# Attention and a top-1 mixture of experts on one core: token rows read in quarters and block-transposed by VectorE, reads on the sync queue, empty slots zeroed ahead

## The chip, the cores and the metric

One core of a Trainium2 chip runs the whole program. The metric is the device time of one execution in microseconds; the kernel before has three such runs. TensorE (PE) multiplies matrices, VectorE (DVE) and ScalarE (ACT) work on elements, GpSimd (POOL) issues the indirect DMAs, whose rows are chosen by an index, and SyncE (SP) issues the plain ones. The engines run side by side, each takes its own instructions in order, and they wait for each other on semaphores.

## The reference

```python
kv  = einsum('bhsd,bhse->bhde', k, v)            # 8 batches, 8 heads, 576 positions, 64 wide
o   = einsum('bhsd,bhde->bhse', q, kv)
o   = o / sqrt(mean(o*o, -1) + 1e-6) * g_norm
x   = o.transpose(0, 2, 1, 3).reshape(4608, 512)  # tokens x channels
logits = x @ w_gate                               # 8 experts
e   = argmax(logits);  p = softmax(logits)[e]
out[t] = p[t] * (relu(x[t] @ w1[e[t]]) @ w2[e[t]])  # w1: 512 x 1024, w2: 1024 x 512
```

Inputs and output are float32. Each token goes to one expert only.

## The kernel before, in words

**Attention.** A loop runs over the eight batches and one round more. A round forms `kv` of its batch (`kv_mm`), transposes the queries on PE (`t_mm`), folds the gate weights into the right operand (`fold_mm`) and copies it to SBUF (`x_copy`). Between these pieces it works on tiles of 128 tokens of the batch pair before: nine tiles a pair, four pairs, 36 tiles. A tile is a product on PE (`o_mm`), the mean of squares on ACT and DVE (`o_red`), its root (`o_nrm`), and the scaling into a row of `xrow` (`o_x`, L676 the rows, L680 the logits). A row is 516 16-bit words: 512 channels in float16, the gate value and the token's number. Row buffers hold three tiles each, and there are four of them.

**Routing.** `route(j, t0, t1)` works on a chunk of tiles of pair j, by generator steps between the tiles of attention. It finds the expert of each token and its place among that expert's tokens, and scatters the rows by an indirect DMA on POOL (L743) into the DRAM array `x_slots`, in which each expert has room for all tokens. The counts go from chunk to chunk.

**Experts.** The slots of an expert are taken in groups of tiles: g0 to g2 are the first three tiles of experts 0 to 2, g3 to g5 the last two tiles of the same, g6 to g10 five tiles each of experts 3 to 7. A spill group for what an expert has beyond its five tiles is put in before the last group, and a loop for still more (`For_i`) at the end has a count that is zero with these inputs. A group is fetched by `fetch`, one indirect gather a tile on POOL (L291), into one of three row buffers `xl`. Slots that no token has taken are out of bounds for the gather, and the buffers were zeroed once at the start. `xpose` turns a tile's four 128x128 blocks on PE (L325), and DVE evicts the result times `g_norm` (L328). `stage1` (L345) takes eight steps of 128 hidden units, with the Relu on ACT (L353); `stage2` (L361) makes one tile of output, DVE scales it by the gate value (L366), and POOL scatters it to the output (L369). The gathers of group r+2 are issued in the first step of stage 1 of group r, and the transposes of r+1 stand between the tiles of stage 2 of r.

**Weights.** Each expert's w1 and w2 come as eight loads of 512 KB on SP's queue (`w_load`, L206 and L210) into four staging buffers, and DVE casts them to float16 (`w_cast`, L220). `w_step` does one cast and one load; its calls are written out by hand between the steps of attention and of the groups.

**Order.** The order of the instructions is that of the program: there is no planner. Buffers come from pools with a number of copies per tag, and the framework puts in the semaphore waits: a tile or DRAM array that is read waits for its writers, and one that is written waits for its readers. `dram_disjoint_views` declares slices whose writers need not wait for each other. The last eight groups are issued by the loop `while unit()`, and the first ones in between attention, from the fourth tile of the last round.

```python
for k in range(cur.K):
    cur.stage2(k)
    if not cur.small:
        w_step()
    while todo and len(todo) > max(cur.K - 2 - k, 0):
        nxt.xpose(todo.pop(0))
```

Of the kernel before, what the change touches and what calls it, by code (L numbers as in the profile page):

```python
# [45 lines left out]
def kernel(  # L46
# [20 lines left out]
    xs_views = dram_disjoint_views(xs.ap(), NT)  # L67
# [9 lines left out]
    for j in range(4):  # L77
# [20 lines left out]
        "w1off": arf[:, None] + 128.0 * np.array([0, 2, 1, 3], np.float32)[None, :],  # L98
# [36 lines left out]
    nc.scalar.dma_start(g2[64:128, :], g_norm.unsqueeze(1))  # L135
    wgt = P_const.tile([128, 8, 8], F32, tag="wgt")
# [17 lines left out]
    chunks = {0: [(0, 9)], 1: [(0, 9)], 2: [(0, 3), (3, 9)], 3: [(0, 3), (3, 6), (6, 9)]}  # L154
    ohbs, n_route = [], 0
    for j in range(4):
# [7 lines left out]
    xl_ring = [  # L164
        P_const.tile([128, SLOT_TILES, ROW], I16, tag=f"xl{n}", name=f"xl{n}") for n in range(3)
    ]
# [13 lines left out]
    def w_load(pool, bufs):  # L180
# [23 lines left out]
        if n < 4:  # L204
            r0 = 128 * (2 * (n % 2) + n // 2)
            nc.sync.dma_start(st, w1[r0 : r0 + 128, :])  # L206
            dst = w_tiles[e][0][:, n, :]
        else:
            m = 2 * (n - 4)
            nc.sync.dma_start(  # L210
                st.rearrange("p (t d) -> p t d", t=2),
                w2[128 * m : 128 * m + 256, :].rearrange("(t p) d -> p t d", p=128),
            )
            dst = w_tiles[e][1][:, m : m + 2, :].rearrange("p t d -> p (t d)")
        w_staged.append((e, dst, st))

    def w_cast(engine):
        if w_staged:
            e, dst, st = w_staged.pop(0)
            engine.tensor_copy(dst, st)  # L220
# [5 lines left out]
    def w_step():  # L226
        if len(w_staged) == 4 or not w_todo:
            w_cast(nc.vector)
# [8 lines left out]
    cnt = P_const.tile([128, 8], F32, tag="cnt")  # L237
    srow = P_const.tile([128, 8, SLOT_TILES], F32, tag="srow")
# [4 lines left out]
    def row_index(name, ctr, ne, nk):  # L243
        bad = P_const.tile([128, ne, nk], F32, tag="bad" + name, name="bad" + name)
        nc.vector.tensor_tensor(
            bad, _bc(cv["srank"][:, 0:nk], 1, ne), _bc(ctr[:, 0:ne], 2, nk), op=ALU.is_ge
        )
        idx = P_const.tile([128, ne, nk], I32, tag="idx" + name, name="idx" + name)
        nc.vector.scalar_tensor_tensor(
            out=idx, in0=bad, scalar=BIG, in1=srow[:, 0:ne, 0:nk], op0=ALU.mult, op1=ALU.add  # L250
        )
        badi = P_const.tile([128, ne, nk], I32, tag="badi" + name, name="badi" + name)
        nc.vector.tensor_scalar(badi, bad, BIG, None, op0=ALU.mult)
        return idx, badi

    rows = {}

    def early_rows():
        ctr = P_const.tile([128, 8], F32, tag="cnt_e")
        b0 = base[len(routed)]  # L260
        nc.vector.tensor_tensor(ctr, b0, cv["ebase"], op=ALU.subtract)
        rows["early"] = row_index("e", ctr, EARLY, EARLY_TILES)
        nc.vector.tensor_tensor(b0, b0, cv["efloor"], op=ALU.max)
        yield
        for i in range(EARLY):
            groups[i].fetch()
        yield

    def final_rows():
        nc.vector.tensor_tensor(cnt, base[n_route], cv["ebase"], op=ALU.subtract)  # L270
        rows["all"] = row_index("a", cnt, 8, SLOT_TILES)

    class Group:
        def __init__(self, n, e, k0, k1):
# [4 lines left out]
            self.xl = xl_ring[n % 3]  # L279
            self.table = "early" if self.small and k0 == 0 else "all"  # L280

# [6 lines left out]
        def fetch(self):  # L288
            idx = rows[self.table][0]
            for k in range(self.K):  # L290
                nc.gpsimd.indirect_dma_start(  # L291
                    out=self.xl[:, k, :], out_offset=None, in_=xs.ap(),
                    in_offset=IndirectOffsetOnAxis(
                        ap=idx[:, self.e, self.k0 + k : self.k0 + k + 1], axis=0
                    ),
                    bounds_check=E * N - 1, oob_is_err=False,
                )

        def slot_ids(self):
            badi = rows[self.table][1]  # L300
# [3 lines left out]
                self.xl[:, 0 : self.K, D + 2 : D + 4].bitcast(I32),  # L304
                badi[:, self.e, self.k0 : self.k0 + self.K].unsqueeze(2), op=ALU.max,
            )

# [6 lines left out]
        def start(self):  # L314
            self.xsT = self.pool().tile(
                [128, 4, self.n], F16, tag="xsT" + self.tag(), bufs=1, name="xsT"
            )

        def tag(self):
            return ""  # L320

        def xpose(self, k):
            ps = PSA.tile([128, 4, 128], F16, tag="KV", bufs=2, name="xps")
            for c in range(4):
                nc.tensor.transpose(  # L325
                    ps[:, c, :], self.xl[:, k, c * 128 : (c + 1) * 128].bitcast(F16), ident16
                )
            nc.vector.tensor_scalar(  # L328
                self.xsT[:, :, k * 128 : (k + 1) * 128], ps, g2, None, op0=ALU.mult
            )  # L330

        def stage1(self, f):
            if f == 0:
                self.hT = self.pool().tile(
                    [128, 8, self.n], F16, tag="hT" + self.tag(), bufs=1, name="hT"
# [7 lines left out]
            for kk in range(4):  # L343
                for hp, s in zip(hps, starts):
                    nc.tensor.matmul(  # L345
                        hp,
                        self.w()[0][:, kk, f * 128 : (f + 1) * 128],
                        self.xsT[:, kk, s : s + self.step],
# [6 lines left out]
        def stage2(self, k):  # L355
            if self.small:
                yp = PSA.tile([128, D], F32, tag="O", bufs=2, name="yp")
            else:
                yp = PSA.tile([128, D], F32, tag="T", bufs=2, name="yp")
            for f in range(8):  # L360
# [6 lines left out]
                y, yp, self.xl[:, k, D : D + 2].bitcast(F32), None, op0=ALU.mult  # L367
# [10 lines left out]
    class SpillGroup(Group):  # L378
        def __init__(self, tables, col, view):
            self.tables, self.col, self.view = tables, col, view  # L380
            self.e, self.K, self.n, self.step, self.small = "s", 1, 128, 128, False

        def tag(self):
            return "d"
# [25 lines left out]

    class LoopGroup(SpillGroup):
# [3 lines left out]
        def fetch(self):  # L415
            super().fetch()
            self.wd = (
# [73 lines left out]
    tabs = []  # L491
# [4 lines left out]
    def ffn():  # L496
        order = list(groups)
        cur = order[0]
# [394 lines left out]
```

## Time and profile before

| what | value |
| --- | --- |
| runs, median (lowest to highest) | 352.06 us (350.06 to 354.91) |
| the profiled execution | 330.94 us |
| its span, first to last instruction | 329.2 us |
| mean granted PE clock | 0.903 |
| busy: PE, DVE, ACT, POOL | 269.0, 183.4, 119.9, 137.6 us |
| stage 1 starts: g0, g1, g2, g3 | 153.1, 169.1, 180.5, 191.7 us |
| stage 1 starts: g6, g7, g8, g9, g10 | 221.9, 240.4, 258.9, 277.3, 302.7 us |

The runs were timed in another session than the profile; the profiled execution is 6% below their median. Sums made from the profile are made against 330.94 us. In the page, a busy time is that of an engine; an idle time is given with what ended it; the clock row is the share of full speed that PE was granted, in forty slices of 8.2 us. A row of groups ends with the idle time ahead of the group and the instruction that released it.

### The profile page before, as it was taken

To read this page: it belongs to the slowest core of one execution; us is meant where nothing else is said; L and a number is where in the kernel's file an instruction comes from. 1 tells how busy PE (TensorE), PEld (TensorE's weight loads), DVE (VectorE), ACT (ScalarE), POOL (GpSimd) and SP (SyncE) were. 2 spreads that over 40 slices of the span, in tenths; PEclk is the share of its full clock that TensorE was granted. 3 is DMA by queue.
4 is the path that set the end of the run, shared out by engine and by line. 5 is a ranking of instruction groups with operands and counts; after the bars stand their busy time and mean duration, and the time that the engine had idled before them with its cause. 6 is when DMAs were issued, how large, how long until landed. Compare 5 with 4: busy or idle time off the path is not lost.

```text
span 329.2 us, 7247 instructions
## 1 busy us (share of the span) xinstructions
PE 269.0 (82%) x2759; PEld 189.3 (58%) x2759; DVE 183.4 (56%) x433; ACT 119.9 (36%) x316; POOL 137.6 (42%) x147
## 2 busy tenths in 40 slices
PE   0699897689766977564979996989999999997980
PEld 0587776577656866462535563657565665645630
DVE  6205566346745368889184678344657658375040
ACT  1136564436543445322322431326142240602600
POOL 9100001720076004384675462777477656052041
PEclk9999997959995589555999998999999999999996
DMA  6999999997897016799589894667799999983021
GB/s 158 334 368 367 369 368 367 381 282 216 246 323 295 18 67 167 250 323 324 201 260 372 295 322 121 214 214 251 250 339 358 351 397 279 408 284 130 0 99 55
DMA packets 45395, 85.79 MB, mean 261 GB/s; under 512 B 6188, under 2 KB 22829, under 8 KB 45360
## 3 DMA queue, kind: packets, MB, share of 16 engines
q1 hardware_dynamic: 36736, 66.07, 59.9%
q0 software_dynamic: 6976, 18.96, 15.6%
q10 hardware_dynamic: 1648, 0.29, 0.5%
q8 instruction: 22, 0.36, 0.4%
q14 instruction: 13, 0.11, 0.1%
HBM read 71.77 MB, written 15.50 MB: 265 GB/s over the span
## 4 chain that ended last, share of the span: by engine, by line
PE 26%; issue 11%; DMA 9%; POOL 7%; DVE 5%; POOLq 1%; ACT 0%; DVEq 0%; ACTq 0%
PE hp L345 13%; PE yp L361 11%; DMA out_dram<-y,d_id 7%; POOL out_dram L369 4%; POOL xl L291 2%; DMA xl<-x_slots,idxe 2%; PE xps L325 1%; DVE y L366 1%; DMA x_slots<-xrow,posi 1%; POOL x_slots L743 1%; DVE w1e L220 1%; DVE xsT L328 0%; POOLq L888 0%; POOLq L854 0%; DVE w2e L220 0%
## 5 line engine op out<-in xcount | busy, mean ns | idle before, releaser
L353 ACT ACTIVATE hT<-hp 128x320 f16<-128x320 f32 (+3 forms) x136 | 53.6, 426 | 106.5 <-PE hp L345 105.9
L345 PE MATMUL hp<-xsT,w1e 128*128 128x320 f16 (+2 forms) x512 | 76.6, 306 | 7.2 <-DVE xsT L328 6.3
L361 PE MATMUL yp<-w2e,hT 128*128 128x512 f16 x320 | 74.1, 379 | 0.3 <-DVE y L366 0.3
L369 POOL DMA_INDIRECT out_dram<-y,idv x40 | 44.6, 1115 | 60.3 <-DVE y L366 49.3
L345 PEld LDWEIGHTS <-w1e 128*128 128x128 f16 x512 | 51.0, 100 | 32.1 <-issue 11.7
L651 PE MATMUL ops<-kvx,qT 64*128 64x72 f32 (+1 forms) x640 | 48.0, 310 | 10.5 <-DVE lhat L680 9.6
L743 POOL DMA_INDIRECT x_slots<-xrow,posi x36 | 35.7, 991 | 40.5 <-DVE xrow L739 15.5
L651 PEld LDWEIGHTS ops<-kvx,qT 64*128 64x128 f32 (+1 forms) x640 | 42.3, 215 | 15.0 <-issue 9.3
L361 PEld LDWEIGHTS <-hT 128*128 128x128 f16 x328 | 30.8, 98 | 31.6 <-issue 0.4
L366 DVE TENSOR_SCALAR y<-yp,xl 128x512 f32<-128x512 f32 x40 | 30.0, 750 | 33.6 <-PE yp L361 29.9
L664 DVE TENSOR_REDUCE ms<-sq 128x8 f32<-128x512 f32 x36 | 24.6, 685 | 25.1 <-ACT sq L660 25.0
L291 POOL DMA_INDIRECT xl<-x_slots,idxa x31 | 32.4, 1046 | 11.7 <-issue 7.0
L594 PE MATMUL kvps<-mk,mv 128*64 128x64 f32 x640 | 28.7, 258 | 9.4 <-DMA mv<-in_v_dram 9.1
L676 DVE TENSOR_TENSOR xrow<-ops,rs 128x512 f16<-128x512 f32 x36 | 24.7, 686 | 18.0 <-DMA x_slots<-xrow,posi 9.3
L660 ACT ACTIVATE sq<-ops 128x512 f32<-128x512 f32 x36 | 21.5, 598 | 31.9 <-PE ops L651 31.5
L594 PEld LDWEIGHTS kvps<-mk,mv 128*64 128x64 f32 x640 | 26.0, 168 | 11.8 <-issue 10.3
L710 POOL COPY xrow<-tokc 128x3 int32<-128x3 int32 x12 | 3.0, 253 | 64.3 <-DVE xrow L676 64.2
L582 PE MATMUL tps<-ctile,mq 128*128 128x128 f32 x144 | 26.9, 320 | 3.5 <-ACT qT L583 1.9
L220 DVE CAST w2e<-wst 128x1024 f16<-128x1024 f32 x32 | 22.3, 704 | 11.4 <-DMA wst<-in_moe_w_dram 11.4
L583 ACT COPY qT<-tps 128x384 f32<-128x384 f32 x48 | 21.9, 473 | 14.4 <-PE tps L582 14.4
L328 DVE TENSOR_SCALAR xsT<-xps,g 128x512 f16<-128x512 f16 x41 | 19.2, 477 | 12.9 <-PE xps L325 12.7
L220 DVE CAST w1e<-wst 128x1024 f16<-128x1024 f32 x32 | 21.6, 688 | 4.5 <-DMA wst<-in_moe_w_dram 4.5
(99 smaller groups left out, 184.1 us busy)
## 6 DMA issues: line engine op xcount, KB each, us to landing
wst<-in_moe_w_dram SPq DMA_DIRECT2D x64, 512.0 KB, 5.8
mq<-in_q_dram SPq DMA_DIRECT2D x16, 576.0 KB, 7.8
mk<-in_k_dram SPq DMA_DIRECT2D x16, 320.0 KB, 7.5
mv<-in_v_dram SPq DMA_DIRECT2D x16, 320.0 KB, 7.3
mk<-in_k_dram SPq DMA_DIRECT2D x16, 256.0 KB, 7.9
mv<-in_v_dram SPq DMA_DIRECT2D x16, 256.0 KB, 7.1
wsts<-in_moe_w_dram SPq DMA_DIRECT2D x8, 512.0 KB, 5.9
out_dram<-y,idv POOLq DMA_INDIRECT x40, 4.9
```

Source lines behind the costliest of these rows:

```text
L220: engine.tensor_copy(dst, st)
L291: nc.gpsimd.indirect_dma_start(out=self.xl[:, k, :], out_offset=None, in_=xs.ap(), in_offset=IndirectOffsetOnAxis(ap=idx[:, self.e, self.k ...
L345: nc.tensor.matmul(hp, self.w()[0][:, kk, f * 128 : (f + 1) * 128], self.xsT[:, kk, s : s + self.step], start=(kk == 0), stop=(kk == 3),)
L353: nc.scalar.activation(self.hT[:, f, s : s + self.step], hp, ACTF.Relu)
L361: nc.tensor.matmul(yp, self.hT[:, f, k * 128 : (k + 1) * 128], self.w()[1][:, f, :], start=(f == 0), stop=(f == 7),)
L366: nc.vector.tensor_scalar(y, yp, self.xl[:, k, D : D + 2].bitcast(F32), None, op0=ALU.mult)
L369: nc.gpsimd.indirect_dma_start(out=self.views(k), out_offset=IndirectOffsetOnAxis(ap=self.ids[:, k : k + 1], axis=0), in_=y, in_offset=Non ...
L582: nc.tensor.transpose(ps[:, c, :], src[:, 128 * m : 128 * m + 128], cv["ident"])
L594: nc.tensor.matmul(kvps[b][64 * y : 64 * y + 64, 2 * u + a, :], main["v", b, u][:, 2 * y + a, c, :], main["k", b, u][:, 2 * y + a, c, :], ...
L651: nc.tensor.matmul(ps[p0 : p0 + 64 * n, y, o0 : o0 + 72], qT[b][hs, a, blk // 2 : blk // 2 + n, :].rearrange("d c p -> d (c p)"), kvx[b][h ...
L676: nc.vector.tensor_tensor(xr[:, 0:D].bitcast(F16).rearrange("p (a h d) -> p a h d", a=2, h=4), xv, _bc(rs2, 3, 64), op=ALU.mult,)
L743: nc.gpsimd.indirect_dma_start(out=xs_views[9 * j + t0 + t], out_offset=IndirectOffsetOnAxis(ap=posi[:, t : t + 1], axis=0), in_=xrow[j, ( ...
```

## The change

1. The gathers on POOL are replaced. `fetch` reads an expert's slots by place: four plain DMAs on SP's queue, each of which brings one quarter of the channels of all rows (pieces of 256 bytes) to 32 partitions, and a fifth that brings gate values and token numbers (`gi`). Since slots that no token has taken are now read too, `pads` writes rows of zeros to them ahead of it, by one indirect scatter a tile on POOL, out of bounds for the slots that are taken.
2. `xpose` is one transpose in 32x32 blocks on DVE for a whole group. w1's rows are loaded in the order that fits (`(p c) f -> c p f`), and the scale by `g_norm` is put into the casts of w1.
3. The early groups' zeroing follows pair 1 (`early_pads`), closed by a small read on POOL's queue (`fence`); the fetches of groups 0 and 1 follow chunk (2, 9), that of group r+2 follows the first tile of stage 2 of group r, and `pads` of group r+3 follows the first step of stage 1 of group r. The transpose of r+1 follows the second tile of stage 2 of r.
4. Pair 2 is routed in chunks (0,6), (6,9) instead of (0,3), (3,9); there are six row buffers instead of four; `x_copy` is on ACT alone; the experts' steps begin with the second tile of the last round; casts in the last two rounds of attention are shared with ACT.
5. The count of the loop at the end is read in stage 1 of g7, and a memset at the end is gone.

```diff
-    chunks = {0: [(0, 9)], 1: [(0, 9)], 2: [(0, 3), (3, 9)], 3: [(0, 3), (3, 6), (6, 9)]}
+    chunks = {0: [(0, 9)], 1: [(0, 9)], 2: [(0, 6), (6, 9)], 3: [(0, 3), (3, 6), (6, 9)]}
...
-            nc.sync.dma_start(st, w1[r0 : r0 + 128, :])
+            nc.sync.dma_start(st, w1.rearrange("(p c) f -> c p f", c=4)[n])
...
+            if engine is nc.scalar:
+                if n < 4:
+                    engine.mul(dst, st, g4[:, n : n + 1])
+                else:
+                    engine.copy(dst, st)
+            elif n < 4:
+                engine.tensor_scalar(dst, st, g4[:, n : n + 1], None, op0=ALU.mult)
+            else:
+                engine.tensor_copy(dst, st)
...
+    def early_pads():
...
+        for g in groups[0:EARLY]:
+            g.pads()
+            yield
+        fence = P_const.tile([1, 4], I16, tag="fence")
+        nc.gpsimd.dma_start(fence, xs.ap()[0:1, D:ROW])
...
     def early_rows():
...
+        groups[0].fetch()
         yield
-        for i in range(EARLY):
-            groups[i].fetch()
+        yield
+        groups[1].fetch()
         yield
...
     def final_rows():
...
+        for n in range(EARLY, EARLY + 2):
+            groups[n].pads()
...
-        def fetch(self):
-            idx = rows[self.table][0]
+        def pads(self):
+            pad = pads[self.table]
             for k in range(self.K):
                 nc.gpsimd.indirect_dma_start(
-                    out=self.xl[:, k, :], out_offset=None, in_=xs.ap(),
-                    in_offset=IndirectOffsetOnAxis(
-                        ap=idx[:, self.e, self.k0 + k : self.k0 + k + 1], axis=0
+                    out=self.pad_views[k],
+                    out_offset=IndirectOffsetOnAxis(
+                        ap=pad[:, self.e, self.k0 + k : self.k0 + k + 1], axis=0
                     ),
+                    in_=zrow, in_offset=None,
                     bounds_check=E * N - 1, oob_is_err=False,
                 )
+        def fetch(self):
+            r0 = self.e * N + 128 * self.k0
+            src = xs.ap()[r0 : r0 + self.n].rearrange("(g b) w -> b g w", b=32)
+            self.xl = self.pool().tile([128, self.n // 32, 128], I16, tag="xl", bufs=2, name="xl")
+            for i in range(4):
+                c0 = 128 * (2 * (i % 2) + i // 2)
+                nc.sync.dma_start(self.xl[32 * i : 32 * i + 32], src[:, :, c0 : c0 + 128])
+            self.gi = P_fe.tile([128, SLOT_TILES, 4], I16, tag="gi", bufs=3, name="gi")
+            nc.sync.dma_start(
+                self.gi[:, 0 : self.K],
+                xs.ap()[r0 : r0 + self.n, D:ROW].rearrange("(k p) w -> p k w", p=128),
+            )
+        def xpose(self):
+            g = self.n // 32
+            self.xT = self.pool().tile([128, g, 4, 32], I16, tag="xT", bufs=2, name="xT")
+            nc.vector.transpose(self.xT, self.xl.rearrange("p g (a c) -> p g c a", c=4))
...
-        def xpose(self, k):
-            ps = PSA.tile([128, 4, 128], F16, tag="KV", bufs=2, name="xps")
-            for c in range(4):
-                nc.tensor.transpose(
-                    ps[:, c, :], self.xl[:, k, c * 128 : (c + 1) * 128].bitcast(F16), ident16
-                )
-            nc.vector.tensor_scalar(
-                self.xsT[:, :, k * 128 : (k + 1) * 128], ps, g2, None, op0=ALU.mult
-            )
...
+            if real == 0:
+                cur.xpose()
             for f in range(8):
                 cur.stage1(f)
                 if f % 2 == 1 if cur.K != 2 else f % 4 == 1:
                     w_step()
-                if f == 0 and 1 <= real and EARLY <= real + 2 < len(groups):
-                    groups[real + 2].fetch()
                 if f == 5:
                     cur.slot_ids()
+                if f == 0 and EARLY - 1 <= real < len(groups) - 3:
+                    groups[real + 3].pads()
...
-                while todo and len(todo) > max(cur.K - 2 - k, 0):
-                    nxt.xpose(todo.pop(0))
+                if k == 0 and 0 <= real < len(groups) - 2:
+                    groups[real + 2].fetch()
+                if k == min(1, cur.K - 1) and 0 <= real < len(groups) - 1:
+                    groups[real + 1].xpose()
...
-            nc.vector.tensor_copy(kvx[b][:, 1], folds[b][1])
+            nc.scalar.copy(kvx[b][:, 1], folds[b][1])
...
-                    [128, 3, ROW], I16, tag="xrow", bufs=4, name=f"xrow{j}{t}"
+                    [128, 3, ROW], I16, tag="xrow", bufs=6, name=f"xrow{j}{t}"
...
-                for _ in range((0, 1, 1, 2)[max(b - 5, 0)]):
+                if b == 6 and n >= 1:
+                    w_load(P_wa, 3)
+                elif b == 7:
+                    w_step(nc.vector if n % 2 else nc.scalar)
+                elif b == B:
                     w_step()
-                if b == B and n >= 3:
+                    w_step(nc.scalar)
+                if b == B and n >= 1:
                     unit()
                     unit()
...
-    with tc.For_i(0, n_more) as it:
+    with tc.For_i(0, n_more[0]) as it:
```

## The prediction

> **What bounds the kernel now.** I read the page first (busy shares, the forty slices, the groups), then the waits of all engines, the waits of SP's queue, the busy time by stage, and the timeline of POOL around the scatters and at the end.
>
> ```profile
> PE 269.0 (82%) x2759; PEld 189.3 (58%) x2759; DVE 183.4 (56%) x433; ACT 119.9 (36%) x316; POOL 137.6 (42%) x147
> ...
> PEclk9999997959995589555999998999999999999996
> DMA  6999999997897016799589894667799999983021
> ```
>
> PE is busy for 82% of the span, but slices 9, 13, 14 and 17 to 19 (66 to 74, 99 to 115 and 132 to 156 us) show half a clock: there attention runs slowly after a hole in PE's work.
>
> ```profile
> L345 PE MATMUL hp<-xsT,w1e 128*128 128x320 f16 (+2 forms) x512 | 76.6, 306 | 7.2 <-DVE xsT L328 6.3
> L361 PE MATMUL yp<-w2e,hT 128*128 128x512 f16 x320 | 74.1, 379 | 0.3 <-DVE y L366 0.3
> L291 POOL DMA_INDIRECT xl<-x_slots,idxa x31 | 32.4, 1046 | 11.7 <-issue 7.0
> L328 DVE TENSOR_SCALAR xsT<-xps,g 128x512 f16<-128x512 f16 x41 | 19.2, 477 | 12.9 <-PE xps L325 12.7
> ```
>
> These are the parts to be exchanged: the two matmul stages hardly wait, the gathers lie on POOL, the evictions of the transposes on DVE.
>
> ```profile
> 220.00:240.00 20.00, 19.99 (x137) 12.10 (x134) 11.31 (x21) 6.12 (x16) 11.98 (x12) 1.00 0.70 230
> 240.00:260.00 20.00, 20.00 (x136) 12.27 (x134) 13.25 (x28) 6.12 (x16) 14.27 (x13) 1.00 0.97 350
> 260.00:280.00 20.00, 20.00 (x138) 12.38 (x137) 12.74 (x22) 7.12 (x19) 12.64 (x11) 1.00 0.98 348
> ```
>
> In the table by stage (PE, PEld, DVE, ACT, POOL, clock, DMA share, GB/s) the five-tile groups are bound by PE, at full clock, with DMA at 0.97 beside it. Five-tile groups begin at 221.9, 240.4, 258.9, 277.3: a pitch of 18.44 us, which is 8.69 for stage 1 and five times 1.95 for stage 2 with its four transposes.
>
> ```profile
> DVE xrow L676 <- DMA x_slots<-xrow,posi: 9.3, 2, 5.0
> ```
>
> Two stalls of attention: the fifth row buffer waits for an older scatter to land, 4.3 and 5.0 us.
>
> ```profile
> 89.86 0.98 POOL L743 DMA_INDIRECT x_slots<-xrow,posi  x1 [7.70 <-DVE xrow L739]
> 91.15 0.96 POOL L743 DMA_INDIRECT x_slots<-xrow,posi  x1 [0.30 <-issue]
> 92.42 0.96 POOL L743 DMA_INDIRECT x_slots<-xrow,posi  x1 [0.31 <-issue]
> ...
> x_slots<-xrow,posi POOLq DMA_INDIRECT x36, 6.4
> xl<-x_slots,idxa POOLq DMA_INDIRECT x31, 5.7
> ```
>
> An indirect DMA takes POOL 1.27 us from one to the next; the scatters land after 6.4 us, the gathers after 5.7.
>
> [...]
>
> **The change part by part.**
>
> (a) PE transposes gone. 0.22 us a tile on PE (1.95 less the 1.73 of eight matmuls): 25 tiles of the long groups give 5.5 us, the six tiles of g3 to g5 1.3, the early ones 2: −9 at most. The evictions (41 x 477 ns) go with them; [...] Pitch 17.35 to 18.75 against 18.44. I take half: −0.4 a group, −3 with the short groups.
>
> (b) The scale by g in the weight casts. Same shape as the 688 ns cast; 0 to +0.5 us each on DVE, which is busy for 13 of 20 us in this stage. Cost nothing, covered by that slack. The casts moved to ACT in attention are covered too: ACT is 36% busy.
>
> (c) Six row buffers for four, and chunks (0,6),(6,9) for the third pair. The stalls of 4.3 and 5.0 go, and perhaps the half clock after them (tiles of 2.9 us become 4 to 5 there): −9 to −16 us at the start of the last pair (123 now). What is late next: the first direct read. It waits for every row of the third pair in DRAM. POOL must issue nine scatters of pair 1 (11.4), nine zeroings (11.4), have them land (about 8 with the fence), nine scatters (11.4) and their landing (6), then the read (6): 54 us from 85 on, so the rows are here at about 139. The transpose of group 0 is put in DVE's order at the sixth tile of the last pair, which without stalls comes at about 121; DVE stands there and, with it, all tiles behind. So most of the gain is handed back: −9 to +3 at the second group's start (169.1 now), taken as −4.
>
> (d) Tail. The last scatter no longer stands behind the loop's branch (4.67 us idle at 325.20): −3.
>
> (e) Zeroing and reads. POOL's count stays: 40 gathers are replaced by 40 scatters of zero rows. SP gets five transfers a group. SP's issue took 0.35 us for 128 rows and 0.61 for 256 pieces in this trace, so about 1.35 for the 640 pieces of a quarter: 5.4 us from the first issue to the fifth. SP carries all weight loads behind it.
>
> What decides is the order of the two. The slot array is guarded as a whole for the read, and the zeroing index is data. By the order of waits in the changed program, zeroing of group r+3 waits until the read of r+1 has landed, and the read of r+2 waits until the zeroing of r+3 has landed. So reads and zeroings take turns, however far ahead they are put: one zeroing and one read per group, each with its landing. The trace before has no such turn. Bounds: zeroing of five tiles is 4 x 1.27 to its last issue plus 2.7 (the landing of the last outputs, where DMA is idle) to 6.4 (scatters under load), 7.8 to 11.5; I take 4.0, since nearly all rows fall outside the bound and are dropped: 9.1. The read is 5.4 to its last issue plus 2.2 (smallest direct loads) to 5.8 (weights): 7.6 to 11.2; I take 11.1, as DMA is at 0.97. Turn of a long group: 15.4 to 22.7, taken 20.2, against 17.4 to 18.7 on PE. With two tiles the zeroing is 1.3 + 4.0 = 5.3, and the read 4 x 0.6 + 5.7 = 8.1.
>
> The short groups g3 to g5 hurt most: PE is through with each in 7.8 us, but the turns behind them belong to later, longer groups. Let read 3 land at t. Read 4: t + 5.3 + 8.1 = t + 13.4. Read 5 (behind the zeroing of five tiles): + 9.1 + 8.1 = t + 30.6. Read 6: + 20.2 = t + 50.8. Reads 7 to 10: t + 71, 91, 111, 131.6. PE would want read 6 at about t + 25. After read 10: [...] 17.4 of PE, 4.5 of y, scatter and landing: t + 160. For t: zeroings 3 and 4 stand in POOL behind group 0's outputs (before the second group's start, about 165), four issues and landing to 174, then the read 8.1: 181 ± 4. End at 341, against the span of 329.2: +12. This sum has (a), (c) and (d) in it already, since PE is no longer the bound: they only move t.
>
> Own time: the profiled execution was 330.94 us, 1.7 more than its span; 343 after. The median of the runs shown, 352.06, is 1.064 times that, so 365.
>
> **Rivals.**
>
> A, the turn is hidden (faster). Landings at their lower ends: turn 15.4, read 6 at t + 36, PE behind by few us only and catching up never needed. Then PE bounds: −4 (c), −3 (a), −3 (d), less a few, or the full −9 of (a) and −9 of (c): span 308 to 321, best guess 317; 338 in the scale of the runs. For it: last outputs land in 2.7 us; zero rows carry few bytes. Against: DMA share 0.97 in this stage, where transfers land in 5 to 6.
>
> B, no difference. Turn of 17.5 to 18.5: the loss at the short groups (some 10) is what (a), (c) and (d) give: 352.
>
> C, worse. Reads hold SP while they wait for zeroings, and the weight loads behind them start late. SP's own waits before were on casts (60.2 us in 19 waits), so it had room; but DMA at 0.97 can't regain what it stands idle. Where SP stands for over 3 us a group (four staging buffers), each further us is paid: at 24 us a turn, 5 x 4 more than my sum: 385.
>
> D, my forecast, the slower side: 355 to 378.
>
> **How the numbers follow.** D 0.46, A 0.28, B 0.14, C 0.12. The forecast is 365, range 336 to 388 (D, B, most of A, the near part of C); D's own is 355 to 378. Within 2%, which is about what a measurement of this kernel can tell from no change, is B: 0.14. Faster 0.28, slower 0.58.
>
> **What would show it.** Right: in the profile after, POOL's zeroings wait for DMA of xl and SP's reads for DMA of x_slots, in turns; PE has a hole of 10 us or more between 200 and 240 ahead of the first long group, and a pitch of about 20 us with stage 1 waiting for the transpose. DVE idle at the first transpose, at 120 to 140. Tail behind the last y under 6 us. Wrong: a pitch of 17.4 to 18.7 with PE full, and zeroings that land in under 3 us; then A holds. If the clock stays at half in attention though the row-buffer wait is gone, (c) is wrong.

## The result, and the profile after

The changed kernel takes 376.6 us (median of four, 372.58 to 378.97) against 352.61 us of the kernel before beside it: ratio 1.0644, interval 1.0512 to 1.0777, so slower. The forecast of 365 had the sign; the loss is 24 us where 13 were forecast.

Both kernels run at one of two levels, which changes from one comparison to another (the kernel before takes 322 to 337 us or 350 to 363, the changed one 343 to 346 or 373 to 379), so a time is compared only with that of the kernel before in the same comparison and a trace only with one of its own level: the profile of before (330.94 us) is of the lower level, the first profile of the changed kernel (372.58 us) of the upper one, and the changed kernel's trace at the lower level comes from e12.

The page of the changed kernel, first profile: busy times, DMA packets, and the groups that took the place of those shown of before.

```profile
PE 273.2 (74%) x2599; PEld 182.6 (49%) x2599; DVE 178.6 (48%) x394; ACT 128.3 (35%) x331; POOL 127.3 (34%) x145
...
DMA packets 72163, 87.18 MB, mean 235 GB/s; under 512 B 33900, under 2 KB 50543, under 8 KB 72129
...
L388 PE MATMUL hp<-xT,w1e 128*128 128x320 f16 (+2 forms) x512 | 87.4, 332 | 29.1 <-DVE xT L352 12.1
L404 PE MATMUL yp<-w2e,hT 128*128 128x512 f16 x320 | 74.3, 387 | 5.7 <-DVE y L409 4.9
L327 POOL DMA_INDIRECT x_slots<-zrow,padall x31 | 32.6, 1050 | 35.7 <-DMA gi<-x_slots 28.1
```

PE has fallen from 82% to 74% of a longer span (to 76% in e12). Stage 1 now waits 12.1 us for the transpose on DVE (stage 1 before: 6.3 for its eviction), and POOL's 31 late zeroings wait 28.1 us for the read of `gi`, the last transfer of a group's read. Packets under 512 bytes went from 6188 to 33900 while the bytes hardly changed (85.79 to 87.18 MB).

The turns, in the timeline of POOL, lower level (e12): the first zeroing of groups 5, 6, 7, 8 and 9, each with what it waited for.

```profile
179.28 0.98 POOL L327 DMA_INDIRECT x_slots<-zrow,padall  x1 [4.54 <-DMA gi<-x_slots]
...
191.71 0.98 POOL L327 DMA_INDIRECT x_slots<-zrow,padall  x1 [4.21 <-DMA gi<-x_slots]
...
205.02 0.98 POOL L327 DMA_INDIRECT x_slots<-zrow,padall  x1 [4.47 <-DMA gi<-x_slots]
...
220.74 0.98 POOL L327 DMA_INDIRECT x_slots<-zrow,padall  x1 [6.54 <-DMA gi<-x_slots]
...
236.03 0.98 POOL L327 DMA_INDIRECT x_slots<-zrow,padall  x1 [6.42 <-DMA gi<-x_slots]
```

Each start is the landing of a read (3 to 7), and the timeline of SP's queue has the read that follows it:

```profile
199.48 1.86 SPq L342 DMA_DIRECT2D xl<-x_slots  x4
...
213.67 1.97 SPq L342 DMA_DIRECT2D xl<-x_slots  x4
...
228.29 2.29 SPq L342 DMA_DIRECT2D xl<-x_slots  x4
```

Zeroing at 205.02, read at 213.67, landed at 220.74, zeroing again: the two alternate, as forecast. A turn of a long group takes 15.3 to 16.7 us, not 20.

Stage starts at the lower level, the kernel before (e1, span 329.8) and the changed one (e12, span 344.0):

| stage 1 of | before | changed | difference |
| --- | --- | --- | --- |
| g1 | 168.6 | 158.3 | −10.3 |
| g3 | 191.2 | 185.1 | −6.1 |
| g6 | 221.7 | 222.8 | +1.1 |
| g7 | 240.2 | 244.4 | +4.2 |
| g8 | 258.6 | 266.9 | +8.3 |
| g9 | 277.1 | 288.6 | +11.5 |
| g10 | 302.5 | 317.7 | +15.2 |
| end | 329.8 | 344.0 | +14.2 |

By the start of g1 the changed kernel is 10 us ahead; from g1 to g6 it gives them back; the long groups lose 14 more. Of the 11 us given back, 4 lie between g2 and g3 (15.0 us against 11.2), where PE waits 3.69 us for a y that stands on DVE behind a cast whose weights are late.

### The profile page after: what moved, and what is told of

Same layout as the page of the kernel before. It is cut to its first block, busy times and chain, and to the rows that moved or that the text cites. A ratio compares the mean times of both kernels' runs of the same rounds, so it can differ in the third digit from the quotient of the medians.

```text
span 370.4 us, 6970 instructions
## 1 busy us (share of the span) xinstructions
PE 273.2 (74%) x2599; PEld 182.6 (49%) x2599; DVE 178.6 (48%) x394; ACT 128.3 (35%) x331; POOL 127.3 (34%) x145
## 2 busy tenths in 40 slices
DMA packets 72163, 87.18 MB, mean 235 GB/s; under 512 B 33900, under 2 KB 50543, under 8 KB 72129
## 3 DMA queue, kind: packets, MB, share of 16 engines
q0 software_dynamic: 7008, 15.08, 11.2%
## 4 chain that ended last, share of the span: by engine, by line
PE 39%; DVE 17%; issue 17%; DMA 11%; ACT 6%; SPq 4%; another core or an unknown queue 2%; POOL 1%; ACTq 1%; DVEq 0%; POOLq 0%
PE hp L388 12%; DMA wst<-in_moe_w_dram 8%; PE ops L724 8%; PE yp L404 7%; PE kvps L667 7%; PE tps L655 3%; DVE xT L352 3%; DVE y L409 3%; DVE ms L737 3%; DVE w1e L227 2%; SPq L342 2%; ACT sq L733 2%; DMA mv<-in_v_dram 1%; ACT hT L396 1%
## 5 line engine op out<-in xcount | busy, mean ns | idle before, releaser
L388 PE MATMUL hp<-xT,w1e 128*128 128x320 f16 (+2 forms) x512 | 87.4, 332 | 29.1 <-DVE xT L352 12.1
L388 PEld LDWEIGHTS <-w1e 128*128 128x128 f16 x512 | 54.1, 107 | 61.0 <-issue 28.2
L412 POOL DMA_INDIRECT out_dram<-y,idv x40 | 42.3, 1056 | 59.0 <-DVE y L409 49.5
L667 PE MATMUL kvps<-mk,mv 128*64 128x64 f32 x640 | 32.5, 253 | 36.6 <-issue 20.4
L409 DVE TENSOR_SCALAR y<-yp,gi 128x512 f32<-128x512 f32 x40 | 29.5, 741 | 49.2 <-PE yp L404 47.2
L667 PEld LDWEIGHTS kvps<-mk,mv 128*64 128x64 f32 x640 | 27.7, 163 | 41.9 <-issue 32.9
L327 POOL DMA_INDIRECT x_slots<-zrow,padall x31 | 32.6, 1050 | 35.7 <-DMA gi<-x_slots 28.1
L227 DVE TENSOR_SCALAR w1e<-wst,g 128x1024 f16<-128x1024 f32 x28 | 21.0, 760 | 18.7 <-DMA wst<-in_moe_w_dram 18.7
L656 ACT COPY qT<-tps 128x384 f32<-128x384 f32 x48 | 22.0, 473 | 14.3 <-PE tps L655 13.5
L229 DVE CAST w2e<-wst 128x1024 f16<-128x1024 f32 x29 | 20.3, 713 | 11.3 <-DMA wst<-in_moe_w_dram 11.3
L655 PEld LDWEIGHTS tps<-ctile,mq 128*128 128x128 f32 x144 | 17.9, 160 | 10.9 <-issue 4.1
```

Source lines behind the costliest of these rows:

```text
L327: nc.gpsimd.indirect_dma_start(out=self.pad_views[k], out_offset=IndirectOffsetOnAxis(ap=pad[:, self.e, self.k0 + k : self.k0 + k + 1], axis=0
L388: nc.tensor.matmul(hp.rearrange("p (g b) -> p g b", b=32), self.w()[0][:, kk, f * 128 : (f + 1) * 128], self.xcols(kk, s), start=(kk == 0) ...
L409: nc.vector.tensor_scalar(y, yp, self.gate(k), None, op0=ALU.mult)
L412: nc.gpsimd.indirect_dma_start(out=self.views(k), out_offset=IndirectOffsetOnAxis(ap=self.ids[:, k : k + 1], axis=0), in_=y, in_offset=Non ...
L655: nc.tensor.transpose(ps[:, c, :], src[:, 128 * m : 128 * m + 128], cv["ident"])
L667: nc.tensor.matmul(kvps[b][64 * y : 64 * y + 64, 2 * u + a, :], main["v", b, u][:, 2 * y + a, c, :], main["k", b, u][:, 2 * y + a, c, :], ...
```

## The experiments

**e1, the kernel before again.** No edit.

> The kernel before, unchanged. Theory (the profile of before is a fair picture): span within 5 us of 329 and the same stage starts; then the 41 us between the two profiles must be the change. Rival (the profile of before was luckier than its runs, which are 20 us longer): span 345 to 355, with stretches in attention where PE waits for nothing that the profile shows, as between 91 and 114 us in the changed kernel.

326.91 us beside 332.62 of the same kernel (ratio 0.9732, 0.9644 to 0.982), profile 331.61, and the stages stand where the profile of before has them, within 2 us. The profile of before is a fair picture of its level. The same kernel against itself came out 2.7% apart here, so differences of less than 3% between ratios are not read below unless a trace shows the place.

**e2, plain zero fill instead of the late zeroings.**

```diff
         for g in groups[0:EARLY]:
             g.pads()
             yield
+        for g in groups[EARLY:]:
+            for k in range(g.K):
+                if g.k0 + k >= EARLY_TILES:
+                    r0 = g.e * N + 128 * (g.k0 + k)
+                    nc.sync.dma_start(g.pad_views[k][r0 : r0 + 128], zrow)
...
-        for n in range(EARLY, EARLY + 2):
-            groups[n].pads()
...
-                if f == 0 and EARLY - 1 <= real < len(groups) - 3:
-                    groups[real + 3].pads()
```

A second small read after the fill closes it for the scatters that follow.

> The changed kernel; zeroing for groups 3 to 10 (31 indirect scatters on POOL) is replaced by 16 plain writes of zeros on SP's queue after pair 1, to the fourth and fifth tiles of each expert (this holds where no expert has over 384 tokens by then, as with these inputs). Reads then wait for no zeroing. Theory (turns of zeroing and reading set the pace): the hole before group 6 goes (PE from group 3 to group 6 in 23 to 26 us instead of 36.6) and the long pitch falls from 23.5 to 17.4 to 19: 25 to 31 us less than the changed kernel, 345 to 352. Rival (SP's five transfers, the 256-byte pieces or the transpose on DVE set the pace): the pitch stays above 20, and at most 10 us are gained.

341.7 us, ratio 1.0224 (1.0103 to 1.0346), where the changed kernel has 1.056 to 1.066. The ratio alone doesn't settle how much is gone, since against e1, which ran beside it, e2 takes 4.5% longer. The traces of the lower level say more: g10 starts at 306.9 us in e2 and at 317.7 in e12, 10.8 us earlier, but the span is only 4 us shorter, since the end after g10's start takes 33.1 us instead of 26.3. The pitch of the long groups g6 to g9 is 18.9, 19.6 and 18.9 us (21.6, 22.5 and 21.7 in e12), at or just over the 17.4 to 19 of the theory. The short groups don't follow it: g3 to g6 still takes 36.8 us (23 to 26 were expected; changed kernel 37.7, before 30.5), with no zeroing to wait for. PE's timeline shows what they wait for now:

```profile
207.78 5.53 PE L396 MATMUL hp<-xT,w1e 128*128 128x256 f16 x32 [2.00 <-DVE xT L360]
220.36 8.85 PE L396 MATMUL hp<-xT,w1e 128*128 128x320 f16 x64 [3.59 <-DVE xT L360]
```

In a group of two tiles the next transpose comes after the second y, that is after PE's last matmul, and nothing covers it: 2.0 us ahead of a short group, 3.59 ahead of the first long one.

How the zeroings cost the long groups is in part in the waits of DVE between 222 and 318 us, first of the changed kernel (e12), then of e2:

```profile
DVE w2e L229 <- DMA wst<-in_moe_w_dram: 11.2, 7, 4.9
DVE w1e L227 <- DMA wst<-in_moe_w_dram: 8.1, 2, 7.6
```

```profile
DVE w2e L229 <- DMA wst<-in_moe_w_dram: 9.0, 7, 2.3
...
DVE w1e L227 <- DMA wst<-in_moe_w_dram: 2.3, 3, 1.5
```

and in the waits of SP's queue and of PE in the same stretch of the changed kernel:

```profile
SPq L342 <- DMA x_slots<-zrow,padall: 20.8, 7, 9.3
...
PE yp L404 <- DVE y L409: 9.6, 6, 2.2
```

SP stands 20.8 us ahead of reads that wait for zeroings, with the weight loads behind it in its queue; DVE stands for weights that come late, up to 7.6 us at once; y stands behind the casts in DVE's order; PE waits 9.6 us for y (4.2 in e2). The other part is PE's clock: after the 6.12 us that PE waits for g6's transpose in e12, stage 1 of g6 takes 11.63 us, with a mean clock of 0.85 from 222 to 244 us; in e2, after 3.59 us, it takes 8.85, as long as that of g8 in e12 (8.86, at a clock of 1.00 from 267 to 289 us).

**e3, no zeroing on POOL at all.** As e2, and the nine early zeroings with their fence become plain writes of slots 352 to 383 of experts 0 to 2:

```diff
-        for g in groups[0:EARLY]:
-            g.pads()
...
+                elif t == 2 and g.small:
+                    nc.sync.dma_start(g.pad_views[k][r0 + 96 : r0 + 128], zrow[0:32])
```

> As e2_static_fill, and the nine early zeroings on POOL are replaced too, by a plain write of slots 352 to 383 of experts 0 to 2 (enough for these inputs). Theory (PE crawls at one instruction in 0.7 us for as long as POOL issues indirect DMAs at that place): POOL's run of 25 us there shrinks by 12, and 8 to 12 us more are gained than in e2. Rival (the crawl has to do with something else[...]): within 4 us of e2 or the crawl as long as before.

341.04 us, ratio 1.0285 (1.0215 to 1.0355): no different from e2. Its comparison was at the lower level, where e2 has no crawl either, so it doesn't test what it was made for. Nor does POOL's shorter run bring the first group forward (132.9, in e2 130.9): the scatters wait 19.9 us for the closing read instead.

**e4, four row buffers.**

```diff
-                    [128, 3, ROW], I16, tag="xrow", bufs=6, name=f"xrow{j}{t}"
+                    [128, 3, ROW], I16, tag="xrow", bufs=4, name=f"xrow{j}{t}"
```

> The changed kernel with four row buffers instead of six. Theory (the row buffers were a stall of attention, as predicted): 5 to 12 us slower than the changed kernel. Rival (DVE waits for the first read anyway, and the crawl hides it): no difference over 3 us.

352.25 us, ratio 1.0528 (1.0427 to 1.0629), against 1.056 to 1.066 of the changed kernel in other comparisons: no loss to be seen. Its trace says otherwise: DVE waits for row buffers again (`xrow`, 13.0 us in two waits), and g2 starts at 178.9 instead of 170.0. That profiled run is the longest of its four (358.83), so the 9 us are an upper end. What six buffers are worth stays open between 0 and 9 us.

**e5, the changed kernel again.** No edit.

> The changed kernel, unchanged, once more. Theory (the crawl of PE between 91 and 114 us belongs to the place of the run and not to the change): no stretch of single matmuls 0.7 us apart in attention, span near 350, ratio to before still 1.04 to 1.07. Rival (the crawl comes from the change): the same hole of 20 us, span near 370.

377.65 us beside 355.64, ratio 1.066 (1.0586 to 1.0735). The rival seemed to hold, the hole is there again; PE's timeline:

```profile
102.65 0.26 PE L667 MATMUL kvps<-mk,mv 128*64 128x64 f32 x1 [1.15 <-issue]
103.37 0.26 PE L667 MATMUL kvps<-mk,mv 128*64 128x64 f32 x1 [0.46 <-issue]
105.47 0.27 PE L667 MATMUL kvps<-mk,mv 128*64 128x64 f32 x1 [1.84 <-issue]
```

These are single matmuls, multiples of 0.7 us apart, released by nothing that the profile shows, while POOL scatters and zeroes. e12 decides on it.

**e6, the transpose earlier.**

```diff
                 if f == 5:
                     cur.slot_ids()
+                if f == 6 and 0 <= real < len(groups) - 1:
+                    groups[real + 1].xpose()
...
-                if k == min(1, cur.K - 1) and 0 <= real < len(groups) - 1:
-                    groups[real + 1].xpose()
```

> The changed kernel; the transpose of group r+1 is put after the seventh step of stage 1 of group r instead of after the second tile of its stage 2. Theory of turns (reads are late): no gain over 4 us, the transpose is still waited for since its read is not there. Rival (the transpose stands in DVE's order behind y and is exposed: 2.0 to 3.6 us a short group, 1.4 a long one): 12 to 16 us less than the changed kernel.

374.74 us, ratio 1.0578 (1.0486 to 1.067), against 1.066 of e5 beside it: within the noise, as the theory of turns has it. In the stretch of the short groups (213 to 252 us) DVE now stands at the transpose for the read:

```profile
DVE xT L352 <- DMA xl<-x_slots: 15.1, 2, 10.8
```

g3 to g6 takes 36.0 us. Moved up, the transpose uncovers the late read.

**e7, fill and early transpose together.** The edits of e2 and e6.

> e2_static_fill and e6_early_transpose together: no zeroing by POOL from group 3 on, and the transpose in stage 1. If both turns and exposed transposes count: pitch of a long group 17.4, short groups under 10, 10 to 15 us less than e2_static_fill, so 0.97 to 1.0 of before. If the transposes were not the rest: within 4 us of e2_static_fill.

363.15 us, ratio 1.0248 (1.0173 to 1.0324). The places follow: g3 to g6 takes 27.7 us (30.5 before), and the first pitch is 17.3 us. So late reads and exposed transposes each hold the short groups by themselves, and only both edits free them. The time does not follow: e7 is no better than e2 by the ratio. What was won is lost twice: g8 to g9 takes 23.9 us, with DVE waiting 4.93, 0.63 and 2.07 us for weights ahead of y and PE 4.68 for y (DMA is busy for 0.99 of the time from 260 to 280 us and for 0.89 from 280 to 300, which leaves the weights little room to come sooner); and the end from g10's start takes 33.2 us where the changed kernel takes 26.0 and the kernel before 26.5.

**e8, the count read at the end.** e7 with `values_load` of the loop's count after the last group.

```diff
-                    n_more.append(
-                        nc.values_load(
...
+    n_more.append(
+        nc.values_load(
```

> As e7_fill_early_transpose, with the count of the last loop read at the end, as in the kernel before. Predicted step (d): 3 us slower than e7. Rival (in the changed kernel the end after the last scatter is 6.5 to 13.6 us instead of 3.0, so nothing was gained there): no slower than e7.

363.28 us, ratio 1.0238 (1.017 to 1.0305), end from g10's start 33.5 us: no difference. Where the count is read is worth nothing.

**e9, reads doubled.** e7 with the four quarters of the long groups read a second time.

```diff
+            if not self.small:
+                xd = self.pool().tile([128, self.n // 32, 128], I16, tag="xd", bufs=1, name="xd")
+                for i in range(4):
+                    c0 = 128 * (2 * (i % 2) + i // 2)
+                    nc.sync.dma_start(xd[32 * i : 32 * i + 32], src[:, :, c0 : c0 + 128])
```

> e7_fill_early_transpose with the four quarter reads of each five-tile group (and of no other) issued a second time into a tile that nobody uses: 5 x 4 more transfers, 12800 more pieces of 256 bytes. Theory (what is left over the kernel before is the cost of the small pieces, since DMA is busy at 0.9 to 1.0 there): each group gets 3 us or more longer, 12 to 25 us in all over e7. Rival (the pieces lie beside the weights and cost nothing): under 4 us.

348.3 us, ratio 1.0698 (1.0659 to 1.0737); e10 beside it, which is e7 but for the end, has 336.38 and 1.0328: 11.9 us, at the low end of the 12 to 25 expected. From g6 to g10 it takes 100.7 us against 87.2: 4.5 us for each of the three reads issued there (of groups 8, 9 and 10). The doubled reads of groups 6 and 7, issued in the short groups, show no cost (g3 to g6 takes 27.5 us in both). DVE's waits for weights in that stretch, doubled first, single second:

```profile
DVE w2es L229 <- DMA wsts<-in_moe_w_dram: 11.6, 3, 9.1
DVE w1e L227 <- DMA wst<-in_moe_w_dram: 10.7, 3, 8.5
```

```profile
DVE w2es L229 <- DMA wsts<-in_moe_w_dram: 6.5, 3, 4.4
DVE w1e L227 <- DMA wst<-in_moe_w_dram: 4.4, 2, 3.1
```

A read of 2560 pieces is on the path, by way of the weights that come later: 0.66 MB would be an estimated 2 us at the 350 GB/s of the long groups before, and a second read costs 4.5. Some 2 us of the 13.5 are PE's own, at a mean clock of 0.90 instead of 0.94. DMA is busy for 0.97 of the stretch, at 286 GB/s (e10: 0.92 at 295), which speaks for the pieces in DMA; SP's time of issue is not separated from it.

**e10, the end as before.** e7 with the pools closed and the count read ahead of the loop.

```diff
+    manual.close()
+
+    n_more.append(
+        nc.values_load(
...
         grp.stage2(0)
-    manual.close()
```

> e7_fill_early_transpose with the loop's end as in the kernel before (the pools closed and the count read ahead of the loop, no memset). Theory (d, as predicted): the last scatter is late again, 3 us slower than e7. Rival (the long end of e7, 13.7 us after the last scatter, goes): 4 to 8 us faster than e7, and level with the kernel before.

336.38 us, ratio 1.0328 (1.0292 to 1.0365). Neither is seen: it is not 4 to 8 us faster, and the ratios differ from e7's by 0.8%, which e1 says not to read. The last scatter waits for 7.92 us, and the end from g10's start takes 34.8 us. With g10 starting at 298.2 (before: 302.5) this kernel is 4 us ahead of the kernel before when its last group starts, and still ends later.

**e11 and e12, both kernels beside each other.** No edits.

> The kernel before once more, for its trace beside that of the changed kernel. Theory (the crawl in attention comes with the place of the run): where its time is 350 to 355 the trace shows single matmuls 0.7 us apart in attention while POOL scatters, worth about 20 us; where it is 325 to 335 there are none. Rival: at 350 to 355 the extra time lies in the experts' part.

> The changed kernel once more, beside e11. Theory: 15 to 25 us longer than e11 on the same chip, with the crawl in both or in neither; the difference from group 3 on is 20 to 35 us and that of attention under 10. Rival: the difference lies in attention.

327.52 us (ratio of the kernel to itself 1.0026, 0.9972 to 1.008) and 344.65 us (1.056, 1.0438 to 1.0683). The comparison fell on the lower level, and the crawl (the single matmuls of e5) is gone from the changed kernel; the same matmuls in its timeline:

```profile
92.93 1.39 PE L667 MATMUL kvps<-mk,mv 128*64 128x64 f32 x40
```

Forty take 1.39 us. e5 and e12, the same program on the same chip, stand 28.8 us apart when group 0 starts (159.7 and 130.9) and 28.3 us at the end: the level lies in attention, up to the first group, and it is not a matter of the chip. The kernel before differs by 25 us between the levels (355.64 and 330.32), so the gap is about as large there; no trace shows it at the upper level, and that it crawls in the same way is an inference. The expected difference from group 3 on (20 to 35 us) is 20 us: from −6.1 to +14.2, at the low end; attention differs by 10 us in the changed kernel's favour.

## Why the prediction was right, and where it was not

**The sign: right. The mechanism: right up to the first long group.** Zeroing and reading wait for each other in turns, PE has a hole ahead of the first long group (6.12 us, where 10 or more were expected), and the transpose is what stage 1 waits for there and in most of the groups before. In the long groups behind it stage 1 waits for no transpose, and the pitch of 21.6 to 22.5 us (about 20 was forecast) has other causes, told below. PE's timeline at the lower level:

```profile
130.86 2.72 PE L388 MATMUL hp<-xT,w1e 128*128 128x384 f16 x8 [17.19 <-DVE xT L352]
...
222.77 11.63 PE L388 MATMUL hp<-xT,w1e 128*128 128x320 f16 x64 [6.12 <-DVE xT L352]
```

The forecast span, on the level of its profile, was 341; e12 has 344.0. The forecast of 365 for the runs used the factor 1.064 between them and the profile, and the runs at that level lost 22 to 24 us and not 14. That part of the miss is in no step of the sum: 28 us of the upper level lie in the changed kernel's attention, and the kernel before is 25 us longer at that level too.

**(c) Attention, size off, and the half clock wrong in part.** The two stalls went, and with them the half clock behind them (66 to 74 and 99 to 115 us before). The last pair's first row is scaled at 98.2 us, in e1 at 121.4: 23 us earlier, where 9 to 16 were forecast. But the clock falls to half later all the same; its row in the page of e12, in slices of 8.6 us:

```profile
PEclk9999999999995555559998989879999999987996
```

Slices 13 to 18 (103 to 155 us) are at half, six slices as in the kernel before, and no row buffer is waited for. That is the sign that the forecast named for (c) being wrong: with the stalls of the row buffers gone, half a clock in the last pair stays. Then all waits for the first read, as described, PE for 17.19 us. What DVE stands at is not the transpose, though, but a cast ahead of it, in its timeline:

```profile
128.43 0.69 DVE L229 CAST w2e<-wst 128x1024 f16<-128x1024 f32 x1 [10.06 <-DMA wst<-in_moe_w_dram]
129.04 1.77 DVE L352 STREAM_TRANSPOSE xT<-xl 128x1536 int16<-128x1536 int16 x1
```

and the weights of that cast are late because SP's queue holds the first read, which waits for the scatters, ahead of their load:

```profile
121.81 1.88 SPq L342 DMA_DIRECT2D xl<-x_slots  x4
...
124.31 0.42 SPq L211 DMA_DIRECT2D wst<-in_moe_w_dram  x1
```

The transpose begins at 129 and not at 139, since POOL's chain began at 77.3 instead of 85 (the first of the two stalls had stood in pair 1) and had the rows there at most 52 us later, instead of 54. So 10.3 us are kept at g1 and not 4.

**The first read of the chain: right.** Read 3 was forecast at 181 ± 4 and landed at 179.3.

**(e) The turn, mis-sized.** Forecast 20.2, measured 15.3 to 16.7. From the first of five zeroings to the next read it is 7.6 to 8.7 us (forecast 9.1): the read starts 2.2 to 3.0 us after the last zeroing's issue, where 4.0 were taken (6.0 us in the last turn, in which DMA is busy for 0.93 of the time). Zeroings that land in under 3 us were a sign of rival A, and in most of the turns it came. The read is 7.1 to 8.4 us from first issue to landing, forecast 11.1: SP's issue of a quarter takes 0.5 us there (1.97 for four), not the 1.35 drawn out from 128 and 256 pieces. The estimate in proportion to the pieces was wrong. So read 4 came at t + 12.4 (forecast 13.4), read 5 at t + 25.7 (30.6), read 6 at t + 41.5 (50.8), read 8 at t + 73.5 (91).

**What made the loss come out nearly right all the same: two errors that cancel.** By its sum, with the author's estimates for the transpose and for the y held up behind it, stage 1 of g6 starts at about 235 us (read 6 at 231.8), that of g10 at about 319, and the end comes at 341: 85 and 22 us. Measured are 222.8, 317.7 and 344.0: 95 and 26 us. The start of g6 is 12 us less than forecast, the two stretches behind it together 14 more; that the span came out within 3 us is luck.

With a turn of 15.3 to 16.7 us rival A would have had PE full from g7 on, and the reads are there: those of g7 and g8 landed at 236.0 and 252.8, 8 and 14 us ahead of their stage 1. What the long groups lose against e1, 14 us from g6 to g10, is something else. From g6 to g7 it is 3.2 us, most of it stage 1 at the lower clock after the hole (11.63 us, in e1 8.86). From g7 to g9 it is 7.3 us, with PE in waits for y behind late weights, as rival C named. From g9 to g10 it is 3.7 us (29.1 against 25.4), at the spill group: its rows are now put in order by two copies on DVE (`d_xo`) ahead of PE's transposes, and PE waits 4.28 us for them. e2 has these 3.7 us too (29.1); the forecast had no term for the spill group, neither for this wait nor for its work on PE.

e2 shows the zeroings' share: without them g6 to g10 takes 86.5 us instead of 94.9, 2.8 less from g6 to g7 and 5.7 less from g7 to g9. The forecast put D and C as alternatives; they act one after the other, D in the short groups and C in the long ones. Why the weights are late has two sides, though. Three stretches of e12, in the columns of the prediction's table by stage (PE, PEld, DVE, ACT, POOL, clock, DMA share, GB/s):

```profile
222.00:244.00 22.00, 19.86 (x103) 11.03 (x103) 11.03 (x15) 6.12 (x16) 12.51 (x12) 0.85 0.64 173
244.00:267.00 23.00, 18.29 (x108) 10.39 (x107) 13.34 (x21) 6.12 (x16) 12.20 (x12) 1.00 0.93 296
267.00:289.00 22.00, 17.97 (x108) 10.37 (x107) 12.85 (x18) 6.12 (x16) 8.89 (x9) 1.00 1.05 322
```

In the first stretch, while SP stands, DMA is busy for 0.64 of the time (0.76 from 222 to 240 us in e1); behind it DMA is full or nearly so (0.93 and 1.05), which leaves little room to regain what it stood idle. But it moves 296 and 322 GB/s here, and 350 and 348 in the kernel before at 0.97 and 0.98. So the transfers are slower too, and e2, in which SP waits for no zeroing, still moves only 334 GB/s from 244 to 278 us, with DMA busy for 0.9 and more in 16 of the 20 slices there. How the late weights divide between the standing queue and the slower transfers no run shows.

**(a) The transposes.** One of 2560 elements takes 2.84 us (2.82 to 2.85 in e12); what the forecast took for it was the author's estimate, which no trace of the kernel before shows. Where one stands between y of tile 1 and y of tile 2, PE stops for 1.4 us (1.38, 1.44 and 1.43 in e2), the whole of the 1.4 us between the forecast's two pitches, of which half was taken, and a long group is 18.9 us in e2 against 18.44 before. Not seen at all was that in the groups of two tiles the transpose is exposed, 2.0 to 3.6 us each; e6 and e7 show it only together, since the late reads covered it.

**(b) The scaled casts.** 760 ns against 688: within the 0 to 0.5 us given, but the cover named for them, DVE's slack, is not free: y waits behind these casts in order when their weights are late (PE 9.6 us for y in e12).

**(d) The tail, wrong.** Forecast −3. From g10's start to the end it is 26.0 us in the changed kernel, 26.5 before. The last scatter is no longer late by 4.67 us, but the end comes 3.5 us later after it (6.5 instead of 3.0 us after POOL's last work). Behind the last y it is 8.0 us in e12, where under 6 were expected, and 8.4 before.

Three things stay open: why the end is 6 to 9 us longer in all kernels with the plain fill (32 to 35 us from g10's start; at the very end of e2 and e7 SP's queue waits 7.9 us for PE's, in the changed kernel 1.7); what the upper level is; what six row buffers are worth. None of the versions beat the kernel before; the nearest, e2, e7 and e8, are 2% behind by their ratios, which is less than e1 lets one tell.

## What to carry to other kernels

When a buffer in DRAM is guarded as a whole, a write ahead for a later group and a read for an earlier one wait for each other, however far ahead either is issued (15.3 to 16.7 us a turn in e12); count one landing for each per turn, and then look at what else stands in the queue behind the waiting read, for here much of the cost showed there (SP stood for 20.8 us, and PE waited 9.6 us for y, in e2 4.2). Where DMA is full beside PE, as in the long groups here (0.93 and 1.05), a read in pieces of 256 bytes can cost more than its size says (in e9 4.5 us instead of an estimated 2 for 0.66 MB at 350 GB/s, SP's issue included), and what PE saves may not be kept. A transpose that replaces another engine's work belongs where its input is there and its engine idle; put after the last y of a short group it is bare (2.0 and 3.59 us in e2). Two waits that end at about the same place must be removed together before either shows (g3 to g6 takes 36.8 us in e2, 36.0 in e6 and 27.7 in e7).

## What the runs showed of the hardware that was not expected

Issuing a quarter took SP 0.49 us with 640 pieces of 256 bytes (g6, four in 1.97 us) and 0.47 us with 256 (g5, four in 1.86 us), less than the loads of k had taken in the kernel before (0.60 us): here the time of issue does not go with the number of pieces. The same program on the same chip ran 28 us apart in two comparisons (e5 and e12), all of it in attention, with PE issuing one matmul in 0.7 us or a multiple of it in the one while POOL issued indirect DMAs, and forty in 1.39 us in the other. And the zeroings, of which only about a sixth of the rows were written (an estimate: their queue moved 15.08 MB, the rows and outputs of 4608 tokens are 14.2 of it, and 40 full tiles of rows would be 5.3), took POOL 1.29 us from one to the next, no less than the scatters that write every row (1.27 us).
